# Values loaded by head, weights read with a stride, dummies before the fold, and tokens as weights in the last window

## The chip, the cores and the metric

The kernel runs on one core of a Trainium2 chip. The metric is device time in microseconds, a median over several runs. The engines are PE (TensorE; its weight loads are listed as PEld), DVE (VectorE), ACT (ScalarE), POOL (GpSimd) and SP (SyncE, which here only issues transfers).

## The reference

Two stages follow each other. The first is linear attention with a polynomial sketch; its output is the token matrix of the second, a layer pair with the activation h - tanh(h).

```python
# q, k, v: (4 batches, 4 heads, 1088 positions, 32); S1, S2: (8, 32); x: (4352, 128)
def phi(x):                                  # 8 x 8 = 64 features
    a = np.einsum('rd,bhsd->bhsr', S1, x)
    b = np.einsum('rd,bhsd->bhsr', S2, x)
    return np.einsum('bhsi,bhsj->bhsij', a, b).reshape(*x.shape[:-1], r * r)
q_p, k_p = (phi(q), phi(k))
kv = np.einsum('bhsf,bhsd->bhfd', k_p, v)
z = np.sum(k_p, axis=2)
num = np.einsum('bhsf,bhfd->bhsd', q_p, kv)
den = np.einsum('bhsf,bhf->bhs', q_p, z)[..., None] + 1e-06
x = (num / den).transpose(0, 2, 1, 3).reshape(B * S, H * D)
h = x @ w_in                                 # w_in (128, 2048)
g = h - np.tanh(h)
return (g @ w_out).astype(np.float32)        # w_out (2048, 128)
```

All inputs and the output are float32.

## The kernel before

*The planner.* The program is a list of operations, each with an engine, an estimated cost and a due time. `schedule` lays them out; the order in which each engine issues its instructions is written out in the table `ORDER` (numbers of operations), so the costs only decide where dummy matmuls go. A dummy (L504 at the start, the same form later) multiplies zeros and is put in where the plan shows PE idle before its next operation: 512 columns wide if that fits, else 128, and only if it ends 60 ns before the operation's planned start. There are 24 of them.

*The loads.* SP issues nearly all transfers, one after the other, each about 0.5 us apart in the queue; an issue may first wait for a semaphore, and what is queued behind it then waits too. The order for the head is: the keys of batch 0 in three loads, the queries of batch 0 in two, the values of batch 0 in four (L480), w_in in four pieces of 512 columns (L488, pieces 0, 3, 1, 2), then piece 2 of w_out (L493), whose issue waits until the values have landed, the rest of the queries, pieces 1, 0 and 3 of w_out, and then the loads of batch 1, the first of which waits for the last piece of w_in. The two 8-row loads of S1 and S2 (`s_raw`) go through ACT's queue. A load of values covers 32 partitions, the rows of a quarter of the positions for all four heads; a piece of w_out is read in rows of 512 bytes, so that partition `ji` holds rows `ji`, `128 + ji` and so on.

*Attention for a batch.* Keys are transposed to kT by DVE (L574), multiplied by the sketch on PE, transposed back to `kab` (L591), and multiplied pairwise to `wk` by POOL and DVE. PE multiplies `wk` with the values (the tiles, L643 for batch 0); ACT copies the result to `kvs` (L649); PE folds it (`fold0`); ACT writes the two halves of `kvb` under a mask `pmask` (L531). The mask of heads, `mask`, comes from a small matmul of a table `e4` that POOL builds (L549), and `s2p` from another (L552). Queries go the same way; their products with `kvb` (the numerators; L677 is a transpose within batch 0's, followed by ACT's copy `qpB` at L684) and the denominators give the tokens, `xT` in bf16.

*The layers.* The 4352 tokens pass in windows: two of 256, seven of 512 and a last one of 256. For each window PE multiplies 16 blocks of 128 columns of w_in with the tokens (L913), ACT takes tanh (L917), and PE adds 16 blocks of w_out times that into bank 0 (`acc`, L926). The h of `h - tanh(h)` is not subtracted: w_in times w_out is folded once to a 128 x 128 matrix (transposes of w_in, L857, the copies `w_inT`, and L870), split in a high and a low bf16 part, `whi` and `wlo`, and two matmuls with the tokens (L898) add the linear part. ACT casts the pieces of w_in to bf16, POOL those of w_out (L844 and L848). A window ends with DVE's 32 x 32 transpose of `acc` to `osb` (L932) and its stores, in runs of 128 bytes. In the last window `osb` is 128 x 256, and its four stores are divided between the queues of SP and ACT, two each.

The weights and the tokens meet like this, in the functions `layers` and `linear_turn`: w_in in blocks of 128 neighbouring columns is PE's stationary operand, the tokens stream; w_out in blocks of 128 rows is stationary, the tanh streams; the result has the 128 outputs on the partitions and the tokens along the row, which is why it is transposed.

On ACT the head's order is: `kvs`, the cast of w_in piece 0, the second and first half of `kvb`, `qpB` and the copies of the numerators, with the other casts between them.

Of the kernel before, what the change touches and what calls it, by code (L numbers as in the profile page):

```python
# [13 lines left out]
R = 8  # L14
# [3 lines left out]
NTOK = B * S  # L18
# [12 lines left out]
COLD = 6800  # L31
CHUNK = 256
# [20 lines left out]
    ),  # L53
    "scalar": (
# [4 lines left out]
    ),  # L59
    "vector": (  # L60
# [5 lines left out]
    ),  # L66
    "gpsimd": (
        "24 16 2 3 4 19 5 25 6 20 7 17 18 79 80 81 110 106 22 23 107 21 109 108 111 150 152 241 242 247 251 363 365 364 370 374 "
        "506 508 507 517 513 "
    ),  # L70
    "sync": (
# [22 lines left out]
class Program:  # L94
# [46 lines left out]
    def schedule(self):  # L141
# [21 lines left out]
        while left:  # L163
# [20 lines left out]
            if e == "tensor":  # L184
                if filling and o in self.fill_stops:
                    filling = False
                if filling and fills_from in order["vector"]:
                    free[e] = max(free[e], fills_from.at + fills_from.cost + 200, 1050)
                    while True:
# [3 lines left out]
                        if free[e] + long + 60 > o.at:  # L193
                            break
# [149 lines left out]
def bass_polysketch_attn__then__act_tanh_shrink_kernel(nc, q, k, v, S1, S2, moe_w_in, moe_w_out, out):  # L344
# [26 lines left out]
    e4 = sb("e4", [4, 4, 4, 8])  # L371
    hmask = sb("hmask", [128, 2])
    pmask = sb("pmask", [128, 2])
    mask = sb("mask", [128, H, R])
# [31 lines left out]
    tt = sb("tt", [128, UNITS, UNIT], BF16)  # L406
    osb = [sb(f"osb{i}", [128, 512]) for i in range(2)]
# [6 lines left out]
    KG = 9 * 32  # L414

# [42 lines left out]
    def load_keys(prio):  # L458
# [9 lines left out]
        for x, (g0, g1, lo, hi) in enumerate(((0, 4, 0, 160), (0, 3, 160, 288), (3, 4, 160, 224))):  # L468
# [33 lines left out]
    def constants():  # L502
# [16 lines left out]
        for h in range(2):  # L519
            P.op("vector", 110, lambda e, h=h: e.memset(pmask[64 * h:64 * h + 64, h:h + 1], 1.0),  # L520
                 w=[("pmask",)], prio=-998)
# [369 lines left out]
    def layers(w, f0, n, widths, hooks):  # L891
# [38 lines left out]
        if not f0:  # L930
            lin()
# [134 lines left out]
```

## Time and profile before

| | |
|---|---|
| median of 3 runs | 107.88 us (107.62 to 108.11) |
| the profiled execution | 107.41 us |
| its span in the trace | 105.6 us |
| granted TensorE clock, mean | 0.996 |
| PE busy | 97.0 us (92%) |
| ACT busy | 78.5 us (74%) |
| DVE busy | 60.4 us (57%) |
| POOL busy | 35.9 us (34%) |

The profiled execution took 1.8 us more than its span; this lies around the instructions. All stamps below are microseconds from the start of the span. A few instants of the head are needed later: `fold0` starts at 11.53, the first layer (L913) at 16.25, the fold of w_in and w_out (L870) at 19.34, and the last matmul ends at 101.97. The profile's page lists busy time by engine, the slices of the span, the DMA queues, the chain of work that ended last, and groups of instructions with what released them; the views of the trace show the same by window, engine or line.

### The profile page before, as it was taken

To read this page: it belongs to the slowest core of one execution; us is meant where nothing else is said; L and a number is where in the kernel's file an instruction comes from. 1 tells how busy PE (TensorE), PEld (TensorE's weight loads), DVE (VectorE), ACT (ScalarE), POOL (GpSimd) and SP (SyncE) were. 2 spreads that over 40 slices of the span, in tenths; PEclk is the share of its full clock that TensorE was granted. 3 is DMA by queue.
4 is the path that set the end of the run, shared out by engine and by line. 5 is a ranking of instruction groups with operands and counts; after the bars stand their busy time and mean duration, and the time that the engine had idled before them with its cause. 6 is when DMAs were issued, how large, how long until landed. Compare 5 with 4: busy or idle time off the path is not lost.

```text
span 105.6 us, 2945 instructions
## 1 busy us (share of the span) xinstructions
PE 97.0 (92%) x1243; PEld 50.2 (48%) x1254; DVE 60.4 (57%) x128; ACT 78.5 (74%) x107; POOL 35.9 (34%) x45
## 2 busy tenths in 40 slices
PE   6899899999999969989899999999999999999960
PEld 2557556774576433423644343544444434345540
DVE  2378966899899999198389546892550020200210
ACT  3340588746768836769899796989969999899930
POOL 5637058710946700884900059176000000000000
PEclk9999999999999999999999999999999999999998
DMA  2999999603841503799202300035013222015263
GB/s 46 288 218 346 321 313 243 239 20 72 261 120 19 151 20 77 189 228 253 73 0 33 51 6 0 6 53 87 0 22 50 46 43 44 0 31 91 36 94 55
DMA packets 26509, 11.21 MB, mean 106 GB/s; under 512 B 19072, under 2 KB 24320, under 8 KB 26496
## 3 DMA queue, kind: packets, MB, share of 16 engines
q1 hardware_dynamic: 25920, 10.95, 42.9%
q8 instruction: 10, 0.16, 0.6%
q10 hardware_dynamic: 576, 0.07, 0.4%
q14 instruction: 3, 0.02, 0.1%
HBM read 8.78 MB, written 2.23 MB: 104 GB/s over the span
## 4 chain that ended last, share of the span: by engine, by line
PE 58%; DMA 12%; DVE 10%; ACT 5%; SPq 4%; POOL 4%; issue 3%; POOLq 0%; DVEq 0%
PE ps L926 21%; PE ps L913 21%; DMA w_out_f<-in_moe_w_out_dram 5%; ACT tt L917 5%; PE ps L821 4%; DMA vx<-in_v_dram 4%; PE ps L898 4%; DMA out_dram<-osb 3%; DVE qpT L804 3%; POOL w_out L848 2%; DVE qp L798 2%; DVE osb L932 2%; SPq L480 2%; PE ps L752 1%; DVE qab L760 1%
## 5 line engine op out<-in xcount | busy, mean ns | idle before, releaser
L917 ACT ACTIVATE tt<-ps 128x1024 bf16<-128x1024 f32 (+1 forms) x70 | 66.9, 998 | 10.9 <-PE ps L913 10.2
L913 PE MATMUL ps<-xT,w_in 128*128 128x512 bf16 (+1 forms) x151 | 40.4, 346 | 1.3 <-issue 0.6
L926 PE MATMUL ps<-tt,w_out 128*128 128x512 bf16 (+1 forms) x158 | 39.7, 347 | 0.2 <-issue 0.2
L630 POOL TENSOR_TENSOR wk<-kab 128x768 f32<-128x768 f32 (+2 forms) x11 | 15.7, 1424 | 22.7 <-DVE kab L591 22.2
L913 PEld LDWEIGHTS ps<-xT,w_in 128*128 128x128 bf16 x160 | 14.0, 97 | 17.5 <-ACT tt L917 5.5
L926 PEld LDWEIGHTS ps<-tt,w_out 128*128 128x128 bf16 x160 | 15.3, 99 | 13.2 <-issue 1.3
L932 DVE STREAM_TRANSPOSE osb<-ps 128x512 f32<-128x512 f32 (+1 forms) x10 | 6.4, 636 | 24.1 <-PE ps L926 22.9
L798 POOL TENSOR_TENSOR qp<-qa,qab 128x768 f32<-128x768 f32 x6 | 11.2, 1867 | 7.3 <-DVE qa L788 7.1
L804 DVE STREAM_TRANSPOSE qpT<-qp 128x768 f32<-128x768 f32 x9 | 8.4, 961 | 4.1 <-POOL qp L798 4.0
L760 DVE STREAM_TRANSPOSE qab<-ps 128x576 f32<-128x576 f32 (+2 forms) x10 | 6.0, 638 | 2.5 <-PE ps L752 2.5
L740 DVE STREAM_TRANSPOSE qT<-qraw 128x576 f32<-128x576 f32 (+2 forms) x9 | 5.8, 653 | 0.0
L504 PE MATMUL ps<-wz 128*128 128x512 bf16 x9 | 4.6, 581 | 1.0 <-DVE hmask L514 1.0
L821 PE MATMUL ps<-qpT,kvw 32*32 32x288 f32 (+1 forms) x192 | 4.6, 398 | 0.8 <-DVE qpT L804 0.8
L570 DVE STREAM_TRANSPOSE kT<-kraw 128x576 f32<-128x576 f32 x6 | 4.4, 746 | 0.0
L831 ACT CAST xT<-ps 128x256 bf16<-128x256 f32 x6 | 2.1, 380 | 2.8 <-PE ps L821 2.8
L898 PE MATMUL ps<-xT,whi 128*128 128x512 bf16 (+1 forms) x10 | 3.5, 353 | 0.7 <-DVE osb L932 0.4
L798 DVE TENSOR_TENSOR qp<-qa,qab 128x768 f32<-128x768 f32 x3 | 4.0, 1346 | 0.1
L848 POOL CAST w_out<-w_out_f 128x512 bf16<-128x512 f32 x4 | 2.4, 611 | 4.5 <-DMA w_out_f<-in_moe_w_out_dram 4.1
L591 DVE STREAM_TRANSPOSE kab<-ps 128x576 f32<-128x576 f32 (+2 forms) x5 | 3.2, 656 | 1.1 <-PE ps L583 1.1
L821 PEld LDWEIGHTS ps<-qpT,kvw 32*32 32x32 f32 x192 | 2.5, 103 | 2.8 <-DVE qpT L804 1.3
L712 PEld LDWEIGHTS ps<-wk,vx 128*32 128x32 f32 x216 | 3.2, 110 | 1.2 <-issue 1.2
L712 PE MATMUL ps<-wk,vx 128*32 128x64 f32 x216 | 3.6, 220 | 0.0
(90 smaller groups left out, 90.1 us busy)
## 6 DMA issues: line engine op xcount, KB each, us to landing
vx<-in_v_dram SPq DMA_DIRECT2D x12, 144.0 KB, 3.6
qraw<-in_q_dram SPq DMA_DIRECT2D x4, 288.0 KB, 4.6
w_in_f<-in_moe_w_in_dram SPq DMA_DIRECT2D x4, 256.0 KB, 4.8
w_out_f<-in_moe_w_out_dram SPq DMA_DIRECT2D x4, 256.0 KB, 5.9
out_dram<-osb SPq DMA_DIRECT2D x16, 64.0 KB, 2.0
kraw<-in_k_dram SPq DMA_DIRECT2D x3, 288.0 KB, 4.2
kraw<-in_k_dram SPq DMA_DIRECT2D x3, 256.0 KB, 4.1
qraw<-in_q_dram SPq DMA_DIRECT2D x3, 256.0 KB, 3.1
```

Of the source, the lines that this page charges most:

```text
L630: P.op(eng, dve(cols) if eng == "vector" else pool2(cols), lambda e, t0=t0, t1=t1, ap=ap, m=m, ka0=ka0: e.tensor_tensor(out=wk[:, t0:t1, : ...
L712: ins = e.matmul(ps[32 * h:32 * h + 32, vb, 0:64], vx[i][:, h, t, :], wk[:, t, h, :, :], start=(t == 0), stop=(t == NT - 1), tile_position ...
L740: P.op("vector", dve(hi - lo), lambda e: e.transpose(out=qT[i][:, lo:hi], in_=qraw[i][:, lo:hi]), r=cells("qraw", i, lo, hi), w=cells("qT" ...
L760: P.op("vector", dve(2 * n), lambda e, h=h: e.transpose(out=qab[:, t0:t1, h:h + 2, :].rearrange("p t h x -> p h t x"), in_=ps[:, qb + h:qb ...
L798: P.op(eng, dve(cols) if eng == "vector" else pool2(cols), lambda e, p0=p0, p1=p1, w=w: e.tensor_tensor(out=qp[:, p0:p1, :, :, :].rearrang ...
L804: P.op("vector", dve(cols), lambda e, p0=p0, p1=p1: e.transpose(out=qpT[:, p0:p1, :, :, :].rearrange("p t h y j -> p (t h y j)"), in_=qp[: ...
L821: ins = e.matmul(ps[32 * h:32 * h + 32, nb[g], 0:32 * n], kvw[i][32 * g:32 * g + 32, y, 32 * h:32 * h + 32], qpT[32 * g:32 * g + 32, t0:t0 ...
L898: P.op("tensor", pe(n), lambda e, x=x: e.matmul(acc[:, 0:n], x[:, :], xT[:, f0:f0 + n], start=f0 > 0 and x is whi, stop=not f0 and x is wl ...
L913: P.op("tensor", pe(n), lambda e, jb=jb + y, y=y, hb=hb: e.matmul(hb[:, n * y:n * y + n], w_in[:, 128 * jb:128 * jb + 128], xT[:, f0:f0 + ...
L917: P.op("scalar", act(q * n), lambda e, un=un, hb=hb, q=q: e.activation(out=tt[:, un, 0:q * n], in_=hb[:, 0:q * n], func=AF.Tanh, scale=-1. ...
L926: P.op("tensor", pe(n), lambda e, jb=jb, un=un, y=y: e.matmul(acc[:, 0:n], w_out[:, jb, :], tt[:, un, n * y:n * y + n], start=(not f0 and ...
L932: P.op("vector", dve(n), lambda e: e.transpose(out=osb[u][:, 0:n], in_=acc[:, 0:n]), r=[ka], w=[("osb", u)], prio=slot0, name=f"osb{w}")
```

## The change

Several things change together:

- *Values of batch 0* (`load_v`): four loads, one for each head, bring the first 27 of 34 position groups to 96 partitions each (3 thirds of 32 rows; the source is walked as 3 x 32 x 288 elements); a fifth brings the remaining 7 groups of all heads to the other 32 partitions. Batch 1 is loaded as before.
- *Queries of batch 0*: the first two loads become one of 512 columns.
- *w_out* is loaded as `(ji jb)`: partition `ji` holds four neighbouring rows, 2 KB in one run. So that both factors meet in the same hidden unit, `hidden` reads every fourth column of the 512 of a w_in piece, for the first layer's weights and for the transposes of the fold.
- *Masks*: `mask` is made by four DVE reductions over `ident`; `e4`, its matmul and the matmul of `s2p` go, the latter being done within the sketch's first PE operation. `kvb` is cleared by POOL once, and ACT copies its diagonal blocks in place of the two masked activations.
- *Dummies*: `EARLY = 5000` allows dummies past the planned start of an operation that is planned before 5 us and ready just then. The program has 35 instead of 24. Thirteen (eleven of 512 columns, two of 128) stand between the tiles and `fold0`.
- *The last window*: tokens and tanh become the stationary operand, in two halves of 128 tokens, and w_out, `whi` and `wlo` stream, 128 wide, into banks 6 and 7. The result has tokens on the partitions. DVE copies one half and ACT the other to `olast`; SP and ACT issue one store each, of rows of 512 bytes. The window's two linear products stand far ahead of its other matmuls.
- *Orders*: the tables for all engines are new. On SP, after the keys come one of the value loads, the queries, the other four value loads, w_in piece 1, piece 1 of w_out (whose issue waits for the values), w_in 0, w_in 2, w_out 0, the rest of the queries, w_out 3, w_in 3, then a value load of batch 1 (which waits for w_in 2), another, w_out 2, and the rest of batch 1. On ACT the cast of w_in piece 0 stands before `kvs`, then come `kvs`, the cast of piece 1, the halves of `kvb`, `qpB`.

The diff, cut to its core:

```diff
 ORDER = {
...
-                        if free[e] + long + 60 > o.at:
+                        if free[e] + long > o.at + (120 if o.at < EARLY and o.at - o.ready < 1 else -60):
                             break
...
+    def hidden(w, jb):
+
+        return w[:, 512 * (jb // 4):512 * (jb // 4) + 512].rearrange("p (i j) -> p j i", j=4)[:, jb % 4]
...
     def load_v(b, prio):
         i = b % 2
-        src = v[b].rearrange("h (j c) d -> j h c d", j=32)
-        for g in range(4):
+        src = v[b].rearrange("h (j c) d -> j h (c d)", j=32)
+        for x in range(0 if b else 4):
+            rows = src[:, x, 0:KG]
+            rows = bass.AP(tensor=rows.tensor, offset=rows.offset, ap=[[KG, 3], *rows.ap])
+            o = load("sync", 128 * 32 * 27, ("vx", i), f"v{i}", prio, lambda e, x=x, rows=rows: e.dma_start(
+                out=vx[i][0:96, x, :, :].rearrange("p t d -> p (t d)"), in_=rows), True, 300)
+            o.lag = 300
+        for g in range(0 if b else 3, 4):
             n = 9 if g < 3 else 7
...
-                in_=moe_w_out[512 * x:512 * x + 512, :].rearrange("(jb ji) c -> ji jb c", jb=4)))
+                in_=moe_w_out[512 * x:512 * x + 512, :].rearrange("(ji jb) c -> ji jb c", jb=4)))
...
+        for g in range(4):
+            P.op("vector", 110, lambda e, g=g: e.tensor_reduce(
+                out=mask[32 * g:32 * g + 32, :], in_=ident[32 * g:32 * g + 32, 32 * g:32 * g + 32].rearrange("p (h i) -> p h i", i=R),
+                axis=AX.X, op=ALU.add), r=[("ident",)], w=[("mask",)], prio=-989, name=f"mask{g}")
+        P.op("gpsimd", 240, lambda e: e.memset(kvb[:, :, :, :], 0.0), w=[("kvb", 0), ("kvb", 1)], prio=-976)
...
-            scaled(kvb[:, :, y, :], ps[:, vb, 0:128].rearrange("p (x y d) -> p x y d", x=2, y=2)[:, :, y, :], pmask[:, y:y + 1], 64,
-                   [bank[vb], ("pmask",)], [("kvb", y)], T["kvb"], f"kvb{y}")
+            P.op("scalar", act(64), lambda e, y=y: e.copy(
+                kvb[64 * y:64 * y + 64, :, y, :], ps[64 * y:64 * y + 64, vb, 0:128].rearrange("p (x y d) -> p x y d", x=2, y=2)[:, :, y, :]),
+                r=[bank[vb]], w=[("kvb", y)], prio=T["kvb"], name=f"kvb{y}")
...
-                ins = e.transpose(out=bv[:, 128 * j:128 * j + 128], in_=w_in[:, 128 * jb:128 * jb + 128],
+                ins = e.transpose(out=bv[:, 128 * j:128 * j + 128], in_=hidden(w_in, jb),
...
-                    hb[:, n * y:n * y + n], w_in[:, 128 * jb:128 * jb + 128], xT[:, f0:f0 + n], start=True, stop=True),
+                    hb[:, n * y:n * y + n], hidden(w_in, jb), xT[:, f0:f0 + n], start=True, stop=True),
...
+            if last:
+                def both(e, jb=jb, un=un, y=y):
+                    for dst, _, at in halves:
+                        ins = e.matmul(dst, tt[:, un, n * y + at:n * y + at + 128], w_out[:, jb, :], start=False, stop=jb == NJB - 1)
+                    return ins
...
+        if last:
+            for y, (eng, queue) in enumerate((("vector", "sync"), ("scalar", "scalar"))):
+                P.op(eng, act(128) if y else dve(128), lambda e, y=y: (e.copy if y else e.tensor_copy)(
+                    olast[:, y, :], halves[y][0]), r=[bank[6 + y]], w=[("olast", y)], prio=slot0, name=f"osb{w}")
+                c = (f0 - (B - 1) * S) // 32 + 4 * y
+                P.op(queue, 65536 / 250, lambda e, c=c, y=y: e.dma_start(
+                    out=ob[B - 1, :, c:c + 4, :].rearrange("j c e -> c j e"), in_=olast[:, y, :]),
+                    r=[("olast", y)], sem=f"outlast{y}", prio=slot0, name=f"out{w}")
+            return
```

More of the change, by code (lines that the diff above doesn't have):

```diff
@@ L31 @@
 COLD = 6800
+EARLY = 5000
 CHUNK = 256
@@ L370, in bass_polysketch_attn__then__act_tanh_shrink_kernel @@
     e16 = sb("e16", [16, 16, 8])
[L371 removed]
     hmask = sb("hmask", [128, 2])
[L373 to L374 removed]
+    mask = sb("mask", [128, H])
     s_raw = sb("s_raw", [16, D])
@@ L535, in put @@
             for h in range(H):
-                ins = e.matmul(ps[32 * h:32 * h + 32, 5, 0:32], s_raw[:, :],
-                               ident[0:16, None, 0:16].to_broadcast([16, 2, 16]),
-                               start=True, stop=True, tile_position=(0, 32 * h))
+                e.matmul(ps[32 * h:32 * h + 32, 5, 0:32], s_raw[:, :],
+                         ident[0:16, None, 0:16].to_broadcast([16, 2, 16]),
+                         start=True, stop=True, tile_position=(0, 32 * h))
+            for h in range(H):
+                ins = e.matmul(ps[32 * h:32 * h + 32, 6, 64:96], e16[:, :, :].rearrange("p a b -> p (a b)")[:, 32 * h:32 * h + 32],
+                               s_raw[:, :], start=True, stop=True, tile_position=(0, 32 * h))
             return ins
-        P.op("tensor", 100, put, r=[("s_raw",), ("ident",)], w=[bank[5]], prio=-3000, mode="32x32", name="psk", ni=16)
+        P.op("tensor", 170, put, r=[("s_raw",), ("ident",), ("e16",)], w=[bank[5], bank[6]], prio=-3000, mode="32x32", name="psk", ni=32)
         for h in range(2):
@@ L548, in folding @@
     def folding():
[L549 to L556 removed]
         for h in range(H):
[L558 removed]
+            scaled(s2blk[:, h, :], ps[:, 6, 64:96], mask[:, h:h + 1], 32, [bank[6], ("mask",)], [("s2blk", h)], -850, f"s2blk{h}")
     KCUT = ((0, 576), (576, NT * 128))
@@ L894, in layers, with both @@
         xs = [("x", b, c // 4, c % 4) for b, lo, m, _ in parts(f0, n) for c in range(lo // 32, (lo + m) // 32)]
+        last = f0 + n == NTOK
+        halves = [(ps[:, 6 + y, 0:128], f0 + 128 * y, 128 * y) for y in range(2)]
         def lin():
             for x, nm in ((whi, "whi"), (wlo, "wlo")):
-                P.op("tensor", pe(n), lambda e, x=x: e.matmul(
-                    acc[:, 0:n], x[:, :], xT[:, f0:f0 + n], start=f0 > 0 and x is whi, stop=not f0 and x is wlo),
-                    r=[(nm,)] + xs, w=[ka], prio=slot0 + LAG - 0.5, name=f"lin{w}")
+                if last:
+                    def both(e, x=x):
+                        for dst, f, _ in halves:
+                            ins = e.matmul(dst, xT[:, f:f + 128], x[:, :], start=x is whi, stop=False)
+                        return ins
+                    P.op("tensor", pe(n), both, r=[(nm,)] + xs, w=[bank[6], bank[7]], prio=slot0 + LAG - 0.5, name=f"lin{w}", ni=4)
+                else:
+                    P.op("tensor", pe(n), lambda e, x=x: e.matmul(
+                        acc[:, 0:n], x[:, :], xT[:, f0:f0 + n], start=f0 > 0 and x is whi, stop=not f0 and x is wlo),
+                        r=[(nm,)] + xs, w=[ka], prio=slot0 + LAG - 0.5, name=f"lin{w}")
         where = []
@@ L938, in layers @@
             for eb in range(4):
-                P.op("scalar" if last and eb % 2 else "sync", 128 * m / 250, lambda e, b=b, c=c, mc=mc, eb=eb, at=at: e.dma_start(
+                P.op("sync", 128 * m / 250, lambda e, b=b, c=c, mc=mc, eb=eb, at=at: e.dma_start(
                     out=ob[b, :, c:c + mc, 32 * eb:32 * eb + 32],
                     in_=osb[u][32 * eb:32 * eb + 32, at:at + 32 * mc].rearrange("p (c x) -> p c x", x=32)),
-                    r=[("osb", u)], sem=f"out{u}s" if last and eb % 2 else f"out{u}", prio=slot0, name=f"out{w}")
+                    r=[("osb", u)], sem=f"out{u}", prio=slot0, name=f"out{w}")
     windows = [(0, 256, (2, 2, 4, 4, 4)), (256, 256, (4, 4, 4, 4))]
```

46 lines of the change are left out of this document (18 added, 28 removed), and 52 rows, old and new, of the table ORDER.

## The prediction

> **What bounds the kernel now.** I read the page's head and its DMA queues, the chain of waits, the windows, the timeline by engine, and SP's waits.
>
> The chain that ended last (start, length in us, what), cut to the head and the end:
>
> ```profile
> 4.70 4.53 DMA vx<-in_v_dram
> 9.25 4.83 DMA w_out_f<-in_moe_w_out_dram
> 14.08 0.05 issue
> 14.13 0.62 POOL w_out L848
> ...
> 19.34 1.07 PE ps L870 x16
> ...
> 99.99 0.66 PE ps L926 x6
> ...
> 102.06 0.45 DVE osb L932
> ```
>
> The head is a chain of loads: the values (vx) land at 9.25, only then SP issues the first piece of w_out, POOL casts, and PE folds the weights (L870) at 19.34. What comes after is a full TensorE. Windows (length, busy us of PE, PEld, DVE, ACT, POOL with counts, clock, DMA share, GB/s):
>
> ```profile
> 9.00:11.80 2.80, 2.80 (x115) 2.03 (x114) 2.36 (x10) 0.59 (x2) 0.94 (x2) 1.00 1.02 347
> 20.40:102.00 81.60, 78.50 (x950) 39.02 (x958) 46.77 (x82) 67.09 (x78) 25.17 (x16) 1.00 0.32 69
> 102.00:105.60 3.60, 0.00 (x0) 0.00 (x0) 0.45 (x1) 0.00 (x0) 0.00 (x0) 0.88 0.48 73
> ```
>
> From 20.4 to 102 PE is busy 78.5 of 81.6 us, so a head that starts that stretch later ends the kernel later by nearly as much. With all 16 DMA engines full (share 1.02) 347 GB/s move: 21.7 GB/s for each engine.
>
> SP's queue in the head and ACT's instructions around kvs (start, length):
>
> ```profile
> 3.27 1.87 SPq L480 DMA_DIRECT2D vx<-in_v_dram  x4
> 5.18 1.85 SPq L488 DMA_DIRECT2D w_in_f<-in_moe_w_in_dram  x4
> 9.25 0.38 SPq L493 DMA_DIRECT2D w_out_f<-in_moe_w_out_dram  x1
> ...
> 11.21 0.27 ACT L649 COPY kvs<-ps 128x128 f32<-128x128 f32 x1 [3.06 <-PE ps L643]
> 11.37 0.62 ACT L844 CAST w_in<-w_in_f 128x512 bf16<-128x512 f32 x1
> 12.06 0.52 ACT L531 ACTIVATE kvb<-ps,pmask 128x64 f32<-128x64 f32 x2
> 13.00 0.77 ACT L684 COPY qpB<-ps 128x256 f32<-128x256 f32 x2 [0.43 <-PE ps L677]
> ```
>
> All four w_in loads are issued before SP stops for the values, and kvs stands ahead of the cast of w_in, so neither shows as a wait. DMA queues of the page (packets, MB, share):
>
> ```profile
> q1 hardware_dynamic: 25920, 10.95, 42.9%
> q10 hardware_dynamic: 576, 0.07, 0.4%
> ```
>
> These tell on how many engines a transfer ran. ACT's queue (q10) carries two s_raw loads of 8 rows (16 data packets) and two of the last stores (32 x 8 runs of 128 bytes each, 512): 528. The 48 left are completions, one per engine taking part: 2 x 16 for the stores leave 8 for each s_raw load. SP's queue (q1) agrees: rows of its 92 transfers make 24448, and 25920 - 24448 = 1472 = 92 x 16. So the only transfers whose outermost count is below 16 ran on just that many engines, 8.
>
> **The change part by part.**
>
> *Values of batch 0 (L480).* Each of the four new loads has 96 rows of 1152 bytes; its source is walked as 3 x 32 rows, outermost count 3. Nothing in the trace has two sides that differ (3 against 96), so the bounds are 3 engines and 16. By the nearest row, s_raw, I take 3. Then 4 x 110,592 bytes go at 3 x 21.7 = 65 GB/s: 6.8 us, and the same three engines also move their sixteenth of q (262,144 bytes, 0.8 us) and of the fifth load (0.3 us): 7.9 us. The keys landed at 5.16, when the second kT transpose (L574) began; the engines are through with them somewhat earlier, about 4.5. Values land at 12.4 instead of 9.25. On 16 engines at 244 (window 4 to 9) to 347 GB/s it would be 8.0.
>
> The Trainium skill, "DMA: Bandwidth & Descriptors", section "Why a DMA increments its semaphore by 16 and not by 1", says that a transfer uses the largest number of engines up to 16 that divides the outermost counts of both sides; the trace agrees for the 8-row loads. By that rule it is 3 here, which gives the sum below, and an even spread gives the first rival.
>
> *SP's order.* One load of w_out (piece 1) still waits for the values, but now w_in 0 and 2, w_out 0, the rest of q, w_out 3 and w_in 3 are queued behind it; only w_in 1 is ahead. w_in 0 goes out one issue (0.48) after 12.4. A load into an empty queue takes 3.2 us to land (the first 320 KB of keys, page section 6), so w_in 0 lands at about 16.0 (before: within 4.8 of 5.2, never waited for).
>
> *ACT's order.* The cast of w_in 0 now precedes kvs: 16.0 + 0.62 = 16.6 instead of 11.21 for kvs, with tiles long done (values at 12.4, then 1.2). Then kvs 0.3, fold 0.5, under which ACT casts w_in 1 (0.6), kvb twice 0.2 (a copy instead of the 0.26 activation), qpB 0.4: the first numerators go at 18.3 instead of 13.43, 4.9 later. Their old slack, 1 us behind the products of DVE (L662, ended 12.46), is used up. From there w_inT twice 0.58, x twice 0.27 and four hops between PE and ACT are as before, 2.8 us: the first layer begins at 21.1 (before 16.25). To the fold of the weights it is less than the old 3.1 us, as fewer matmuls precede it, and the old 0.34 wait for POOL's casts goes; its last piece of w_out, issued after w_in 2 and two value loads, is cast at about 22.5. I take 23.5 for 19.34: +4.2, and 0.4 regained from PE's 3.1 us of gaps up to 102: **+3.8**.
>
> *w_out in 2 KB rows.* Its four loads stop being 512-byte rows (landing 5.9 us against 4.8 for w_in); that saves up to 2.5 us of queue, but the queue is empty from about 6 to 13 us, so nothing of it is on the path: 0. Without the stall it is worth 0.5 (in the first rival).
>
> *Weights with stride 4.* No strided weight load is in the trace. LDWEIGHTS of contiguous bf16 takes 97 ns, of f32 141 ns (L677). Beside a 512-wide matmul (216 ns apart) either is hidden; beside the 48 of 256 (109 apart) 32 ns too much would cost 1.5 us, and 16 transposes up to 1.4. Same bytes per column pass, so I take 0; bounds 0 and 2.9.
>
> *Mask, s2p, kvb.* Two e4 steps on POOL, two f32 PE groups (0.63 each) and one ACT copy go, four short DVE reductions (0.19) come, hidden behind DVE's 2.2 us wait for the keys. 0; without that cover 0.8.
>
> *Dummies.* 35 instead of 24, thirteen of them between tiles and fold: 11 x 0.22 + 2 x 0.06 = 2.5 us at full clock. Tiles end at 13.6, so they end at 16.2, under the wait for kvs (16.9). Cost 0 to 0.8 if the clock is down for part of it; **+0.3**. An earlier warm clock gains nothing while PE waits for the values.
>
> *The end.* Each 256-wide matmul of the last window becomes two of 128. Sixteen such with their weights took 1.07 us (L870), 0.056 apart: 2 x 0.056 - 0.109 = 3 ns each, 18 times: 0.05. Two parallel copies of 0.29 replace the 0.45 transpose (-0.2) and each queue has one issue instead of two (-0.4). But the stores' outermost count is 4: two of 64 KB on 4 engines, 87 GB/s, take 1.5 us instead of 0.4 at 16: +1.1. Net **+0.5** (bounds -0.6 and +1.1).
>
> Sum: 3.8 + 0.3 + 0.5 = 4.6. The profiled execution took 107.41 (span 105.6 and 1.8 around it), so 112.0; the median of the three is 0.47 above it, and on its scale 107.88 + 4.6 = **112.5**.
>
> **The rivals.**
>
> *The loads spread over 16 engines (not slower).* Values at 8.0, w_in 0 at 11.6, kvs at 12.2. The dummies then decide: tiles end at 10.9, 2.5 us of dummies hold the fold until 13.4 (before 11.53); numerators +1.2, of which the faster w_out and the missing POOL wait give back 0.9 and PE's gaps up to 102 another 0.2; end -0.6: -0.5, 107.4, between 106.7 (POOL's wait and w_out worth 1.6) and 108.3 (worth nothing). It decides if transfers go by partitions (96, 128) rather than by the source. For it: in every other load of 16 or more rows all engines took part. Against it: s_raw.
>
> *A cold PE.* PE has nothing from about 9 to 12.4. The first four dummies were 0.43 apart ((1.89 - 0.61)/3, at 1 us), later 512-wide matmuls 0.216. If the idle stretch brings the slow spacing back, thirteen dummies take 4.9 us, to 18.4, against 16.9 for kvs: +1.5, and it decides once they average over 0.27. 114.0. For it: the gap is the longest on PE. Against: in this trace PE never idles so long, so no row shows a fall before the end (0.88 in the last window).
>
> The Trainium skill, "TensorE: Matmul & The Clock Gate", Part 1, states that the clock halves after an idle window of about 3.4 us that runs freely; by that, a 3.4 us gap may or may not fill one, so it supports this rival only in part. The slices show no such fall here while PE worked.
>
> *Slow strided weights.* Another +2.9 at most: 115.
>
> **How the numbers follow.** Forecast 112.5 with chance 0.50, own range 110.3 to 113.6 (values 1 us earlier or later, stores at either bound). Spread over 16 engines 0.32: both sides of s_raw count 8, so it cannot tell what 3 against 96 does. Cold PE 0.14, strided weights 0.04. 106.9 to 113.9 holds nearly all of the first rival and leaves out 0.02 of it, the upper half of the cold PE (0.07), the strided weights (0.04) and the forecast's tails (0.05). About 0.5% is what this measurement can tell from no change: 107.3 to 108.4. The first rival, with its middle at the lower of these marks, is faster 0.16, same 0.13, slower 0.03; all others are slower: 0.71.
>
> **What would show it.** Right: vx landing near 12.4, SP's w_out issue after it with w_in behind; ACT waiting for w_in_f before its first cast; L877 near 23.5; two last stores landing over 2.5 us after issue. On q1, 13 completions fewer for each of the four loads. Wrong: values landing by 8 to 9, kvs released by PE's tiles or hidden by the dummies. If PE idles before L877 with casts long done, I have mispriced POOL; if L931's spacing at 256 is over 0.11, the stride costs.

## The result, and the profile after

| | before | changed |
|---|---|---|
| median of 4 runs | 107.75 us (106.87 to 108.11) | 115.42 us (115.06 to 115.67) |
| profiled execution | 107.41 us | 115.06 us |
| its span | 105.6 us | 113.2 us |

The ratio is 1.072, with a 95% interval of 1.065 to 1.079: 7.7 us slower. The forecast was slower by 4.6, its range ended at 113.9. Times are medians over all runs of a kernel, while a ratio leaves out runs over 1.5% above the fastest of their kernel.

The chain of waits of the changed kernel (start, length, what), where the old one showed values at 9.25 and the fold of the weights at 19.34:

```profile
6.00 6.93 DMA vx<-in_v_dram
12.95 0.33 SPq L504
...
15.70 7.07 DMA w_in_f<-in_moe_w_in_dram
22.77 0.05 issue
22.82 0.63 POOL w_in L851
...
25.06 0.71 POOL w_out L855
25.77 0.05 issue
25.82 1.07 PE ps L877 x16
```

The values land at 12.95, and the fold of the weights starts at 25.82, 6.5 later than before. The windows (length, busy us of PE, PEld, DVE, ACT, POOL with counts, granted clock, DMA share, GB/s):

```profile
9.40:12.70 3.30, 0.00 (x0) 0.00 (x0) 0.83 (x3) 0.00 (x0) 0.59 (x1) 1.00 0.22 76
12.80:16.10 3.30, 3.12 (x106) 2.34 (x106) 1.33 (x6) 0.00 (x0) 0.00 (x0) 0.50 0.62 182
...
18.70:25.80 7.10, 6.19 (x86) 3.96 (x84) 3.48 (x8) 5.13 (x13) 3.93 (x7) 1.00 1.05 269
26.90:108.50 81.60, 80.51 (x982) 42.24 (x980) 46.53 (x82) 67.54 (x79) 25.22 (x16) 1.00 0.31 68
...
111.10:112.00 0.90, 0.00 (x0) 0.00 (x0) 0.00 (x0) 0.00 (x0) 0.00 (x0) 0.85 0.25 67
```

Read them by the DMA share. While PE waits for the values it is 0.22, little more than 3 of 16 engines (0.19), moving 76 GB/s where the old kernel moved 347. In the last 0.9 us in which data still move it is 0.25, 4 of 16. Right after PE's idle stretch the clock is granted at half for 3.3 us. From the end of the fold on, 81.6 us pass up to the last matmul; before they were 81.6 too. So the loss lies in the head, 6.5, and behind the last matmul, 1.0 (4.9 from the start of the last one to the end of the span, before 3.9).

The DMA queues of the page:

```profile
q1 hardware_dynamic: 23792, 10.95, 39.7%
q10 hardware_dynamic: 164, 0.07, 0.2%
```

SP's rows make 22,400 (24,448 of before, less 128 for the merged query load, 1536 for w_out, 384 for a last store of 128 long rows in place of two of 256). The 1392 left are the completions of 91 transfers: 86 x 16, four value loads with 3 each, the last store with 4. ACT's queue: 16 + 128 rows, 2 x 8 completions for s_raw and 4 for its store. This agrees with the rule of the Trainium skill, "DMA: Bandwidth & Descriptors", section "Why a DMA increments its semaphore by 16 and not by 1", for 3 against 96 and for 4 against 128.

PE and POOL in the head (start, length, instruction, in brackets the idle time before and who ended it):

```profile
12.98 0.66 PE L649 MATMUL ps<-wk,vx 128*32 128x64 f32 x16 [3.64 <-DMA vx<-in_v_dram]
...
14.66 1.68 PE L649 MATMUL ps<-wk,vx 128*32 128x64 f32 x56
16.27 2.55 PE L515 MATMUL ps<-wz 128*128 128x512 bf16 x11
18.66 0.28 PE L516 MATMUL ps<-wz 128*128 128x128 bf16 x2
18.77 0.44 PE L658 MATMUL ps<-ident,kvs 128*128 128x128 f32 x2
```

```profile
22.82 0.62 POOL L851 CAST w_in<-w_in_f 128x512 bf16<-128x512 f32 x1 [1.98 <-DMA w_in_f<-in_moe_w_in_dram]
23.57 2.20 POOL L855 CAST w_out<-w_out_f 128x512 bf16<-128x512 f32 x3
```

The tiles, begun at 12.98, end at 16.3, where the prediction gave them 1.2 us; the dummies then run at full speed (2.55) but hold `fold0` until 18.77, although `kvs` was ready at 17.25. And POOL casts three pieces of w_out only after piece 3 of w_in, which landed 7.07 after its issue.

The end (queues of SP and ACT):

```profile
107.19 1.95 SPq L973 DMA_DIRECT2D out_dram<-osb  x4
109.18 0.66 SPq L964 DMA_DIRECT2D out_dram<-olast  x1
```

```profile
108.52 0.27 ACT L961 COPY olast<-ps 128x128 f32<-128x128 f32 x1 [0.52 <-PE ps L947]
108.82 0.64 ACTq L964 DMA_DIRECT2D out_dram<-olast  x1
```

The same of the kernel before:

```profile
102.06 0.45 DVE L932 STREAM_TRANSPOSE osb<-ps 128x256 f32<-128x256 f32 x1 [2.52 <-PE ps L926]
102.54 0.89 ACTq L939 DMA_DIRECT2D out_dram<-osb  x2
```

In the changed kernel DVE's copy was done at 108.81, as ACT's was; SP's store starts 0.37 later, since SP still issues stores of the window before.

### The profile page after: what moved, and what is told of

Read it like the earlier page. It is cut to its first block, busy times and chain, and to the rows that moved or that the text cites. A ratio compares the mean times of both kernels' runs of the same rounds, so it can differ in the third digit from the quotient of the medians.

```text
span 113.2 us, 3019 instructions
## 1 busy us (share of the span) xinstructions
PE 101.5 (90%) x1287; PEld 54.7 (48%) x1287; DVE 60.3 (53%) x129; ACT 77.8 (69%) x107; POOL 35.6 (31%) x44
## 2 busy tenths in 40 slices
DMA packets 23969, 11.21 MB, mean 99 GB/s; under 512 B 17940, under 2 KB 21140, under 8 KB 23956
## 4 chain that ended last, share of the span: by engine, by line
PE 55%; DMA 16%; DVE 9%; SPq 7%; ACT 5%; POOL 2%; issue 1%; POOLq 0%; DVEq 0%
PE ps L931 20%; PE ps L952 19%; DMA w_in_f<-in_moe_w_in_dram 6%; DMA vx<-in_v_dram 6%; ACT tt L935 4%; PE ps L828 4%; DMA out_dram<-osb 4%; SPq L486 3%; PE ps L916 2%; DVE qpT L811 2%; DVE qab L767 2%; DVE qp L805 2%; POOL w_out L855 2%; PE ps L947 2%; PE ps L759 1%
## 5 line engine op out<-in xcount | busy, mean ns | idle before, releaser
L931 PE MATMUL ps<-xT,w_in 128*128 128x512 bf16 (+1 forms) x160 | 42.3, 350 | 0.2
L952 PE MATMUL ps<-tt,w_out 128*128 128x512 bf16 (+1 forms) x144 | 37.6, 356 | 0.0
L931 PEld LDWEIGHTS ps<-xT,w_in 128*128 128x128 bf16 x160 | 16.3, 115 | 14.4 <-ACT tt L935 4.3
L952 PEld LDWEIGHTS ps<-tt,w_out 128*128 128x128 bf16 x144 | 13.8, 99 | 13.2 <-issue 2.2
L968 DVE STREAM_TRANSPOSE osb<-ps 128x512 f32<-128x512 f32 (+1 forms) x9 | 5.8, 645 | 21.5 <-PE ps L952 13.4
L515 PE MATMUL ps<-wz 128*128 128x512 bf16 x21 | 7.5, 484 | 1.0 <-DVE hmask L523 1.0
L851 ACT CAST w_in<-w_in_f 128x512 bf16<-128x512 f32 x2 | 1.2, 619 | 8.4 <-DMA w_in_f<-in_moe_w_in_dram 8.4
L649 PE MATMUL ps<-wk,vx 128*32 128x64 f32 x72 | 2.3, 312 | 3.6 <-DMA vx<-in_v_dram 3.6
L691 DVE COPY qpB<-ps 128x512 f32<-128x512 f32 (+1 forms) x4 | 2.3, 589 | 3.5 <-PE ps L684 3.4
```

Of the source, the lines that this page charges most:

```text
L515: P.filler = (lambda e: e.matmul(ps[:, FB, 0:512], wz[:, :], wz[:, None, :].to_broadcast([128, 4, 128]), start=True, stop=True), wzero, la ...
L931: P.op("tensor", pe(n), lambda e, jb=jb + y, y=y, hb=hb: e.matmul(hb[:, n * y:n * y + n], hidden(w_in, jb), xT[:, f0:f0 + n], start=True, ...
L952: P.op("tensor", pe(n), lambda e, jb=jb, un=un, y=y: e.matmul(acc[:, 0:n], w_out[:, jb, :], tt[:, un, n * y:n * y + n], start=(not f0 and ...
L968: P.op("vector", dve(n), lambda e: e.transpose(out=osb[u][:, 0:n], in_=acc[:, 0:n]), r=[ka], w=[("osb", u)], prio=slot0, name=f"osb{w}")
```

## The experiments

Eighteen runs, each compared with the kernel before on the same chip. Ratios are to that.

**Values on 16 engines (e1), the old end (e2), both (e3), a busy PE (e4).** e1 takes each of the first four loads of 32 partitions:

```diff
-            rows = bass.AP(tensor=rows.tensor, offset=rows.offset, ap=[[KG, 3], *rows.ap])
-                out=vx[i][0:96, x, :, :].rearrange("p t d -> p (t d)"), in_=rows), True, 300)
+        for g, h0, h1 in () if b else ((0, 0, 4), (1, 0, 4), (2, 0, 2), (2, 2, 4)):
+                out=vx[i][32 * g:32 * g + 32, h0:h1, :, :].rearrange("j h t d -> j h (t d)"),
+                in_=src[:, h0:h1, KG * g:KG * g + KG]), True, 300)
```

> The changed kernel; only the source of batch 0's first four value loads differs: each covers 32 partitions (outermost count 32 on both sides), two of them all four heads and two of them two heads. If the three engines are the cause, values land between 8.0 and 9.3 instead of 12.93, the granted clock stays at 1.00 between 12 and 16 us, the fold of the weights starts at 19 to 20 instead of 25.8, and the time is 108.0 to 109.2 (the last stores still on 4 engines). If the new orders and the thirteen dummies cost by themselves, values come as early but the fold of the weights stays above 21.5 and the time above 110.5.

111.47 us, ratio 1.031 (1.022 to 1.039). Over half of the loss went, so the three engines are a cause; what is left is as the second forecast had it. Values land at 9.38, nearly as early as before; ACT's cast of w_in 0 waits until 13.83 and lets `kvs` go at 14.36; the first fold starts at 15.56, the fold of the weights at 21.90, 2.6 later than before. The clock fell here too:

```profile
9.00:12.00 3.00, 2.60 (x107) 2.00 (x107) 2.10 (x10) 0.00 (x0) 0.44 (x1) 0.80 0.40 108
12.00:15.00 3.00, 3.00 (x13) 1.16 (x10) 2.02 (x9) 1.17 (x3) 0.00 (x0) 0.63 0.86 275
```

```profile
8.51 0.38 PE L612 MATMUL ps<-zm,s2blk 128*128 128x32 f32 x2 [0.70 <-DVE zm L608]
...
11.99 3.61 PE L514 MATMUL ps<-wz 128*128 128x512 bf16 x11
```

So the dummies took 3.61 here, where they took 2.55 in the changed kernel. No long idle stretch came ahead of this fall, at 10.8: after PE's first matmul its longest wait was the 0.70 shown. What brought it stays open. The rest points to the order of SP, which has w_in 0 behind its wait; e5 to e8 try this.

> The changed kernel; only the last window is done as before the change (256-wide, transposed, two stores of 64 partitions' worth on each of two queues, 16 engines each). If the stores' four engines are what the end costs, the time from the last matmul to the end of the span goes from 4.7 back to 3.6 to 3.8 and the kernel to 114.2 to 114.6. If the end is late because SP is still issuing the stores of the window before it, only 0.3 or less is gained: 115.1 or more.

> The two edits of the first two runs together. If both prices add up, 107.0 to 108.1, no different from the kernel before within half a per cent. If the rest of the change (2 KB rows of w_out, fewer steps for the masks, more dummies) gains on its own, below 107.0; if the strided weights or the dummies cost, above 108.3.

```diff
-            if last:
-                def both(e, jb=jb, un=un, y=y):
...
-        if last:
-            for y, (eng, queue) in enumerate((("vector", "sync"), ("scalar", "scalar"))):
...
-                P.op("sync", 128 * m / 250, lambda e, b=b, c=c, mc=mc, eb=eb, at=at: e.dma_start(
+                P.op("scalar" if last and eb % 2 else "sync", 128 * m / 250, lambda e, b=b, c=c, mc=mc, eb=eb, at=at: e.dma_start(
```

In e2 and e3 the last window is 256 wide and transposed as before, its linear products back just ahead of the rest. 116.09 (1.076) and 112.08 (1.037): no gain. The time from the start of the last matmul to the end of the span did fall, from 4.9 to 3.6; but the last matmul came 84.0 and 83.7 after the start of the fold of the weights, instead of 82.4 in the changed kernel. The accumulator in bank 0 must first be read by the transpose of the window before, which the new order has late (in e2 the linear product waited 1.33 us for it). So within the new order the new window saves PE about 1.5 and gives 1.3 of it back in the stores; alone, neither price can be read off the time.

```diff
+                if o.name == "tiles.0":
+                    for _ in range(16):
+                        f = Op("tensor", 0, self.filler[0], 0, None, None, "fill")
```

> The changed kernel with sixteen more dummies of 512 columns ahead of the first tiles, so that PE works while the values are awaited (9.3 to 12.9). If the fall of the clock to 0.62 between 12 and 15 us is what made the fold of the attention 1.9 later than forecast, and PE is the bound from there on, the first fold starts at 17.1 to 17.4 instead of 18.77 and the time falls by 1.2 to 1.6, to 113.8 to 114.2. If the third piece of w_in, cast by POOL ahead of three pieces of w_out, sets the fold of the weights anyway (25.8), the clock stays at 1.00 and the time gains 0 to 0.5: 114.9 to 115.4. If the clock falls all the same, nothing changes.

116.61 us (115.18 to 117.11), ratio 1.077 (1.068 to 1.085): no gain. In the profiled run, of 117.11 us, the tiles were fast (0.43 and 0.99, where the changed kernel has 0.66 and 1.68), the clock stayed at 1.00 until 25.7 and the first fold came at 17.71; but the loads of w came up to 2 us later than in the changed kernel, for no reason that the edit explains, and the fold of the weights at 28.28.

**SP's wait and the dummies.** e5 drops the dependence of w_out 1 on the values, so that the wait stands at w_out 3 (in e6 with the values on three engines); e7 leaves out the thirteen dummies of e1; e8 does both to e1.

```diff
+        for o in order["sync"]:
+            if o.name == "load wo1":
+                o.deps = {d for d in o.deps if d.name != "load v0"}
...
-                        if free[e] + long > o.at + (120 if o.at < EARLY and o.at - o.ready < 1 else -60):
+                        if o.name == "fold0" or free[e] + long > o.at + (120 if o.at < EARLY and o.at - o.ready < 1 else -60):
```

> The kernel of e1_v16 (values on 16 engines), and the wait for the values moved on SP from piece 1 of w_out to piece 3, behind w_in 0, w_in 2 and w_out 0, so that these are issued at once. In e1_v16 the dummies between the tiles and the first fold ended at 15.5, the cast of w_in 0 let kvs go at 14.36. If the order of SP is the cost, w_in 0 lands at 11 to 12 instead of 13.76 and the time falls by 2 or more, to 109.5 or less. If the thirteen dummies hold the first fold by themselves, it starts at 14.5 to 15.6 as before and the time falls by 0.2 to 0.9: 110.6 to 111.3.

> The changed kernel with the same move of SP's wait, values still on three engines. If what is queued behind the wait is the cost, 112.5 or less. If the three engines are busy until 12.9 with the values and every later transfer needs them too, w_in 0 lands no earlier than 13.2, the values no later than before, the first fold stays at 18.8 (slow tiles and dummies), and only the 0.6 that the fold of the weights waits for POOL is gained: 114.6 to 115.3.

> The kernel of e1_v16 without the thirteen dummies between the tiles and the first fold. If the dummies are the cost, the first fold starts at 14.6 instead of 15.56, the fold of the weights 0.9 earlier than 21.9, and the time falls by 0.8 to 1.0: 110.5. If the pieces of w that SP sends late set the fold of the weights (the last piece of w_out is cast at 21.2), nothing is gained: 111.1 to 111.6.

> Both: values on 16 engines, SP's wait moved, no thirteen dummies. If late pieces of w and dummies together are all that is left of the head's loss, the first fold starts at 12.0 to 12.6, the fold of the weights at 18.8 to 19.6 (before the change 19.34), and the time is 108.0 to 109.0, 1.0 to 1.5 of loss left in the last stores and none elsewhere. If the strided weights or the other edits cost, 109.5 or more.

| | time | ratio | `kvs` | first fold | fold of the weights |
|---|---|---|---|---|---|
| before | | | 11.21 | 11.53 | 19.34 |
| e1 | 111.47 | 1.031 (1.022 to 1.039) | 14.36 | 15.56 | 21.90 |
| e7 | 111.24 | 1.037 (1.031 to 1.044) | 13.86 | 14.17 | 21.55 |
| e5 | 109.95 | 1.024 (1.020 to 1.029) | 12.04 | 13.99 | 20.32 |
| e8 | 108.70 | 1.012 (1.007 to 1.016) | 11.61 | 11.92 | 20.20 |

e7 gained nothing. Its first fold came 1.4 earlier, but matmuls behind it were slow (four transposes took 1.06, in e1 0.60), so that the first layer came only 0.3 earlier, and PE went on to the fold of the weights without a wait. e5 came out between the two forecasts, 0.7% below e1 though the intervals overlap, and the dummies held the first fold 1.7 past `kvs`:

```profile
11.50 2.55 PE L517 MATMUL ps<-wz 128*128 128x512 bf16 x11
13.88 0.28 PE L518 MATMUL ps<-wz 128*128 128x128 bf16 x2
13.99 0.44 PE L660 MATMUL ps<-ident,kvs 128*128 128x128 f32 x2
```

e8 met its time, though not its fold of the weights (20.20 for 18.8 to 19.6: the cast of the last piece of w_out began only at 19.44). So of the 3% that e1 left, 2% were SP's wait and the dummies together; the dummies alone gave nothing, and 1.2% once the wait was moved (e8 against e5). With the values on three engines the move of the wait gained nothing: e6 took 117.3 us (115.4 to 117.7, against 107.5 for the kernel before, too scattered for an interval). In the profiled run, of 117.65 us, the values even came later, at 14.84. SP had issued pieces of w behind them from 7.04 on; whether these held the values up on the same three engines is not shown:

```profile
14.84 0.66 PE L652 MATMUL ps<-wk,vx 128*32 128x64 f32 x16 [5.62 <-DMA vx<-in_v_dram]
```

**What e8 still lost.** e9 undoes stride and rows; e10 splits the last window into even and odd tokens, so that a store walks 8 groups of 16 rows; e11 sends all pieces of w ahead of the values of batch 1, with no wait for those of batch 0. e12 is the kernel before with the new value loads alone.

```diff
-        return w[:, 512 * (jb // 4):512 * (jb // 4) + 512].rearrange("p (i j) -> p j i", j=4)[:, jb % 4]
+        return w[:, 128 * jb:128 * jb + 128]
...
-        halves = [(ps[:, 6 + y, 0:128], f0 + 128 * y, 128 * y) for y in range(2)]
+        halves = [(ps[:, 6 + y, 0:128], f0 + y, y) for y in range(2)]
-                            ins = e.matmul(dst, xT[:, f:f + 128], x[:, :], start=x is whi, stop=False)
+                            ins = e.matmul(dst, xT[:, f:f + 255:2], x[:, :], start=x is whi, stop=False)
-                    out=ob[B - 1, :, c:c + 4, :].rearrange("j c e -> c j e"), in_=olast[:, y, :]),
+                    out=ob[B - 1, y::2, c:c + 8, :].rearrange("j c e -> c j e"), in_=olast[:, y, :]),
...
-38 43 37 39 42 41 45 40 48 49 44 50 46
+38 43 37 39 42 41 40 45 44 48 49 50 46
-            if o.name == "load wo1":
+            if o.name in ("load wo1", "load wo2", "load wo3"):
```

The first pair is e9 (with w_out read as before the change), the next three are e10, the last two e11. For e12 `load_v` of the diff stands in the kernel before, and the numbers in its order are moved on by the one load more.

> The kernel of e8_v16_free (values on 16 engines, SP's wait moved, no thirteen dummies; 108.7) with the weights back to contiguous blocks: w_out in 512-byte rows, the first layer and the transposes reading 128 neighbouring columns. If stride and rows are worth nothing together, 108.3 to 109.1. If reading every fourth column costs PE time, 108.2 or less, with weight loads of the first layer back at 97 ns from 115. If the 2 KB rows help the head, 109.2 or more, w_out landing 0.5 or more later.

109.57 us, ratio 1.0115 (1.007 to 1.017), against 1.012 for e8: stride and rows together are worth nothing that shows, to within about 0.7 us. The strided weight loads are longer, 115 ns (e8, the first line) against 97 (e9), but lie under the matmuls:

```profile
L933 PEld LDWEIGHTS ps<-xT,w_in 128*128 128x128 bf16 x160 | 16.2, 115 | 14.2 <-ACT tt L937 4.6 <-issue 0.9 <-ACT xT L840 0.7
```

```profile
L933 PEld LDWEIGHTS ps<-xT,w_in 128*128 128x128 bf16 x160 | 14.1, 97 | 15.2 <-ACT tt L937 4.4 <-DVE qab L769 0.9 <-issue 0.9
```

> The kernel of e8_v16_free with the last window's tokens split in even and odd ones instead of two neighbouring halves, so that each of the two last stores walks 8 groups of 16 rows (outermost count 8) instead of 4 groups of 32. If the two stores share four engines now and eight then, their data take 1.0 instead of 1.9 and the time falls by 0.7 to 1.0, to 107.7 to 108.0; the end after the last matmul from 4.9 to 4.0. If the end is set by something else (issue, completion), 108.4 or more.

108.66 us. The kernel before took 108.25 us beside e9 to e12 and 107.49 beside e8, so ratios are compared, for e9 too: 1.002 (0.998 to 1.006), some 1.0 us less than e8. In its profile the time behind the start of the last matmul falls from 4.9 to 4.05, and the share in the last stretch is 8 of 16 engines, at twice the speed of the changed kernel:

```profile
105.30:105.70 0.40, 0.00 (x0) 0.00 (x0) 0.00 (x0) 0.00 (x0) 0.00 (x0) 1.00 0.53 151
```

> The kernel of e10_st8 with all pieces of w_in and w_out ahead of the values of batch 1 on SP and no wait for the values of batch 0 among them. In e8_v16_free the fold of the weights waited 0.8 for the last piece of w_out (cast at 19.44). If that wait passes on to the end, the fold starts at 19.2 to 19.6 and the time is 0.4 to 0.8 below e10_st8: 107.0 to 107.5, no slower than the kernel before. If PE has other gaps behind it, it equals e10_st8.

107.91 us, ratio 0.993 (0.989 to 0.998): this version beats the changed kernel and is at least level with the one before. How much faster it is stays unsure: its twelve runs spread from 106.84 to 111.53, and between the medians of all runs the gain is 0.3%. The fold of the weights starts at 18.86, and in the profiled run `fold0` stands at 11.54, as before.

> The kernel before with batch 0's values alone loaded as the changed kernel does (four loads of 96 partitions, the source walked as 3 x 32 rows, and a remainder); nothing else differs. If the three engines alone cost the 4 us that e1_v16 gave back, values land at 12.6 to 15 instead of 9.23, the first fold starts 3.5 to 5.5 later, and the time is 111.5 to 113.5. If they only hurt together with the changed order of SP, below 110.

113.14, ratio 1.045 (1.040 to 1.050). The value loads alone make the old kernel 4.9 us slower; PE waits 4.14 for them, and its tiles are slow here too (2.15 where they took 1.23); the first fold starts at 17.06, with only the old four dummies ahead of it:

```profile
14.26 2.15 PE L650 MATMUL ps<-wk,vx 128*32 128x64 f32 x72 [4.14 <-DMA vx<-in_v_dram]
```

**What the forecast missed in the head.** f1 leaves the thirteen dummies out of the changed kernel, f2 issues w_in 3 behind w_in 2 and the last piece of w_out ahead of the values of batch 1, f3 does both. f4 and f5 put twelve dummies under the wait for the values instead, on top of f3 and f1. f6 is the changed kernel again.

```diff
-38 43 37 39 42 41 45 40 48 49 44 50 46
+38 43 37 39 40 42 41 45 44 48 49 50 46
...
+                if o.name == "tiles.0":
+                    for _ in range(12):
+                        f = Op("tensor", 0, self.filler[0], 0, None, None, "fill")
```

The first pair is f2, the last lines f4 and f5; the dummies are left out as in e7.

> The changed kernel without the thirteen dummies ahead of the first fold, nothing else. The first fold starts at 17.2 to 17.5 instead of 18.77 either way, held by the cast of w_in 0. If the slow clock and the dummies are what the forecast missed, the fold of the weights starts 1.3 to 1.6 earlier and the time is 113.7 to 114.2. If the late third piece of w_in and POOL's casts behind it set it, it stays at 25.5 to 26.0 and the time at 115.0 to 115.5.

> The changed kernel with w_in 3 issued right behind w_in 2 and the last piece of w_out ahead of the values of batch 1, all still behind SP's wait; dummies and values as in the changed kernel. POOL's last cast then ends at 23.5 to 24.5 instead of 25.8. If loads and casts are what the forecast missed, the time falls by 1.2 or more, to 114.2 or less. If the late first fold (18.8) leads PE to the fold of the weights at 25.0 to 25.3 anyway, 114.7 to 115.2.

> Both edits. If each cause covers for the other, the fold of the weights starts at 23.5 to 24.5 (the forecast's 23.5) and the time falls by 1.4 to 2.2, to 113.2 to 114.0, though f1 gave nothing and f2 no more than 0.7. If it only adds what f1 or f2 gave alone, that one is the cause. If nothing moves, a third thing holds PE.

> f3 (no thirteen dummies, earlier w loads) with twelve dummies of 512 columns ahead of the first tiles, under the wait for the values. If the slow clock after PE's idle stretch is what kept f3 from gaining, the clock is 1.00 from 13 to 22, the first fold starts at 17.2 to 17.6, the first layer at 21.3 to 22.0 instead of 23.2, the fold of the weights at 24.3 to 25.2, set by POOL's casts, and the time is 0.5 to 1.5 below f6. If it equals f3 within 0.4, the clock isn't the third thing.

> f1 (no thirteen dummies, loads as in the changed kernel) with the same twelve dummies under the wait. With the clock kept up, the first layer starts at 21.3 to 22.0, and the fold of the weights waits 1 or more for the third piece of w_in and POOL's casts, at 25.5 to 26.3: within 0.5 of f6. If it is 1.0 or more below f6, the loads don't matter.

> The changed kernel again, unedited, as the mark for f4 and f5: 115.0 to 116.2.

| | ratio | first fold | first layer | fold of the weights |
|---|---|---|---|---|
| f6 (changed) | 1.0735 (1.070 to 1.077) | 18.85 | 22.93 | 26.30 |
| f1 | 1.067 (1.061 to 1.073) | 17.42 | 23.73 | 26.23 |
| f2 | 1.074 (1.068 to 1.079) | 20.39 | 24.48 | 26.72 |
| f3 | 1.064 (1.058 to 1.070) | 17.51 | 23.23 | 25.47 |
| f4 | 1.061 (1.047 to 1.074) | 17.82 | 22.97 | 25.64 |
| f5 | 1.0715 (1.060 to 1.083) | 17.37 | 22.44 | 25.20 |

f1 and f2 each gained nothing that is sure (f2, at 116.39 us, came out above both of its forecasts), f3 about 1% against f6, with intervals that just touch. Neither f1 nor f2 took its cause away in full. In f2 POOL's last cast ended at 25.9, not at 23.5 to 24.5: its first cast waited for a piece of w_out until 21.3, in the changed kernel until 19.2. The clock was at half until 19.1 there, so the dummies ran slowly and held the first fold until 20.39. Without the dummies the slow speed goes on into the work: from the first fold to the first layer 6.3 us pass in f1 and 5.7 in f3, 4.1 in f6. Four transposes (L684) take 1.06 at the slow speed and 0.60 at the full one, here in f3:

```profile
18.10 1.06 PE L684 MATMUL ps<-ident,qp 128*128 128x128 f32 x4
```

In f1 they took as long, though the granted clock is recorded there as 1.00 (in the window's row the figure ahead of the DMA share):

```profile
18.00:21.00 3.00, 3.00 (x17) 2.05 (x17) 0.17 (x1) 1.45 (x5) 0.89 (x3) 1.00 0.96 312
18.01 1.06 PE L684 MATMUL ps<-ident,qp 128*128 128x128 f32 x4
```

So a recorded 1.00 does not prove full speed; the length of a known matmul tells more.

f4 and f5 met their times (0.9 and 0.15 us below f6), but not the steps that were to lead there. PE stayed fast for the tiles, and then idled again, 2.65 us in f4, as ACT held `kvs` for the cast of w_in 0; and the clock fell after that, in f4:

```profile
13.06 0.43 PE L654 MATMUL ps<-wk,vx 128*32 128x64 f32 x16 [1.52 <-DMA vx<-in_v_dram]
...
14.18 0.99 PE L654 MATMUL ps<-wk,vx 128*32 128x64 f32 x56
17.82 0.49 PE L663 MATMUL ps<-ident,kvs 128*128 128x128 f32 x2 [2.65 <-ACT kvs L660]
```

```profile
15.00:18.00 3.00, 0.35 (x13) 0.18 (x3) 2.61 (x13) 1.02 (x3) 0.00 (x0) 1.00 0.79 227
18.00:21.00 3.00, 2.87 (x19) 1.94 (x19) 0.00 (x0) 1.87 (x7) 0.00 (x0) 0.65 0.98 333
```

Two runs of f4 had a mean granted clock of 0.998 and took 113.40 and 113.61 us, two had 0.976 and 0.973 and took 114.99 and 115.14. That may be the price of the fall, but it is not shown: only the run of 114.99 has a trace, f1 took 115.55 to 115.88 at 0.951 and at 0.994 alike, and a run of f6 at 0.998 took 114.86 where one at 0.980 took 114.84.

## Why the forecast was right and wrong

- *Three engines.* Right: values at 12.95 where 12.4 was forecast, three completions for each load, and e1 and e12 show the price from both sides, 4 us gained and 4.9 lost.
- *SP's order and ACT's.* Right: w_in 0 was cast at 16.46, `kvs` copied at 16.99, where the text had 16.0 for the landing and 16.6 for `kvs`. That the order costs even with early values (e1, e5, e8) was not seen: the first rival gave 107.4 for loads on 16 engines, and e1 took 111.5. Its step that failed is "tiles end at 10.9, 2.5 us of dummies hold the fold until 13.4" with values at 8.0 and w_in 0 at 11.6: the values came at 9.4, w_in 0 at 13.8, and the slow dummies held the fold until 15.56.
- *The dummies, "+0.3".* Here the sum failed first. `fold0` started at 18.77 instead of 16.9. The clock was down from 12.8 to 16.1, so the tiles ended at 16.3 and not at 13.6, and full-speed dummies followed them. The rival of a cold PE named the cause and gave it 0.14; it put the slow speed on the dummies, for 1.5. That the wait leaves the tiles slow is shown by e4, f4 and f5: with dummies under the wait the tiles took 0.43 and 0.99, in the changed kernel 0.66 and 1.68. By the Trainium skill, "TensorE: Matmul & The Clock Gate", Part 1, the clock is halved after an idle window of about 3.4 us, which runs freely. This run and its repeat f6 agree (3.64 and 3.46 idle, then half clock); but in f4 the fall followed 2.65 idle us, and in e1 none over 0.70, so a long idle stretch is not the only thing that brings it.
- *The fold of the weights, "cast at about 22.5 ... I take 23.5".* Here it failed a second time: POOL's last cast ended at 25.77. I gave the load of w_in 0 3.2 us into an empty queue (it took 3.1), but w_in 3, the seventh issue of the burst behind the wait, took 7.07, and POOL casts it ahead of three pieces of w_out. These two causes stand side by side in the trace: PE was free for the fold of the weights at 25.25, POOL at 25.77, both late for 23.5, and it started 2.3 late. What each would cost without the other stays open. f1 and f2 did not take their cause away, f3 with both edits brought the fold of the weights to 25.47, and in f4 it came at 25.64 and PE waited 0.26 for POOL.
- *"0.4 regained from PE's gaps".* Wrong: from the start of the fold of the weights to the last matmul 82.4 us passed, before 82.3.
- *The end, +0.5.* Mis-sized: +1.0. The term of +1.1 for four engines held (share 0.25, and e10): behind the end of the last issue 3.4 us passed, before 2.2. The gain of 0.4 for one issue less did not come: from the end of the copies to the end of the last issue 1.0 passed, before 0.9, because SP's store queued behind those of the window before.
- *Stride and rows, 0.* Right (e9, to within 0.7 us), for the two together; they weren't tried apart. *Masks, 0*: not tried.

In sum: the fold of the weights came 6.5 late and not 4.2 + 0.3, 0.1 was lost behind it and not 0.4 regained, the end cost 1.0 and not 0.5: 7.6 in the span, 7.7 between the medians, for 4.6. What made the kernel slower is shown step by step: the ratio goes from 1.072 to 1.031 with the values on 16 engines (e1), to 1.012 with SP's wait moved and the dummies gone (e8), and to 1.002 with the stores on eight engines (e10). How the 2.3 us by which the fold of the weights missed its forecast divide between PE and the loads is not.

## What to carry to other kernels

Look at the outermost counts of both sides of every load that is rewritten: here a source walked as 3 x 32 rows ran on three engines, and a load that was queued behind it on all 16 waited as well (w_in 1, issued at 6.52, landed at 13.6). An issue that waits belongs behind every load whose consumer heads an in-order queue (e8, where the dummies went too). A stretch in which PE waits can cost more than its length: look at the length of the matmuls that follow (tiles 2.15 instead of 1.23 in e12). Filling one wait is not enough if another follows it (f4).

## What the runs showed of the hardware

- Transfers on few engines use the same ones: the two last stores moved 67 GB/s together on four engines in the last 0.9 us of data (share 0.25), 151 on eight (0.53, e10); a piece of w_in issued behind the values at 6.52 landed at 13.6, where w_in 0 took 3.1.
- After 3.6 us without matmuls the clock was granted at half for some 3.4 us although PE was working again; how late it rises again depends on the run and perhaps on what PE does (16.1 in the changed kernel and 19.1 in f2, with dummies behind the tiles, 21.6 in f3 without).
- The clock also fell without such a stretch: in e1 at 10.8, with no wait of PE over 0.70 us between its first matmul and the fall.
- The granted clock can be recorded as 1.00 while matmuls run slowly: in f1's head (four L684 in 1.06, 0.60 in the changed kernel), and in the changed kernel ahead of the wait for the values (two L613 from 8.73 in 0.61; the same two took 0.38 in e1).
